# Two PSUM banks for MLP outputs and two for attention tiles, and w_out loaded right behind w_in

## The chip, the cores and the metric

The kernel runs on one core of one Trainium2 chip. The metric is the device time of one execution in microseconds; the median of several executions counts. The core has a matmul engine (TensorE, PE in the profile), VectorE (DVE), ScalarE (ACT), GpSimd (POOL) and SyncE (SP), which here issues all DMAs in one queue. Each engine takes its own instructions in the order in which they were written.

## The reference

Two layers in a row. The first is a linear attention with a decay per channel, for 4 sequences of 768 steps and 8 heads of 48 channels; the second is an MLP over its 3072 rows of 384 values.

```python
for t in range(S):                                  # attention, per batch b and head h
    cur = np.einsum('bhd,bhe->bhde', u[None] * kt, vt)
    y[:, :, t] = np.einsum('bhd,bhde->bhe', rt, state + cur)
    state = wt[:, :, :, None] * state + np.einsum('bhd,bhe->bhde', kt, vt)
x = attn_out.transpose(0, 2, 1, 3).reshape(B * S, H * D)
h = x @ w_in                                        # 384 -> 2048
r = np.maximum(h, 0.0)
g = s * (r * r) + b
return (g @ w_out).astype(np.float32)               # 2048 -> 384
```

## The kernel before

**Tiling.** The steps are cut into chunks of 128, so there are 24 chunks: chunk n is steps `n // 4` of sequence `n % 4`, and they are done in this order. Two chunks make one MLP tile T of 256 rows, so there are 12 tiles. Matmuls run in bf16 with sums in fp32.

**A chunk of attention** is a row of small steps that go from engine to engine. Its r, k, v, w come by four DMAs (`load`). ACT takes the logarithm of w (`ln`); PE sums it along the steps (`cum`, bank pair A); ACT takes the exponents (`expo`, and `lam` for the state); VectorE multiplies r and k by them (`mult`, tile `prd`); PE transposes (`trans`, a bank of pool B), ACT copies the result out (`tevac`, tile `RK`); PE forms the 128x128 products (`mt`, bank pair A), VectorE masks them (`mask`); PE sums the output (`ymm`, pool B) and the state's increment (`dmm`, pool B); VectorE adds the diagonal part (`yevac`, tile `x_sb`) and the state (`supd`); PE transposes x (`xtr`, pool B) and ACT copies it (`xevac`, tile `xT`). GpSimd prepares the diagonal part, v in bf16 and the state's scale.

**A tile of the MLP** is eight groups of MLP-in (`g1`, six matmuls each into one of two h banks), a relu on ACT (`relu`, a ring of four `rh` tiles), a square (`square`, on ACT or VectorE by the letters of `SQE`, and on VectorE for the first two tiles), and eight parts of MLP-out (`g2`, four matmuls each; four parts fill one o bank), which VectorE evacuates with s and the bias term (`oevac`). The bias term, b times the column sums of w_out, is made once: 16 matmuls (`colsum`, tile `cs_ps`, an o bank) and a copy on ACT (`bconst`).

**PSUM** has eight banks: A takes two, B three, h two, o one.

**Weights** come in four pieces of w_in and four of w_out, 768 KB each, in fp32, and are cast to bf16 by the engines that the letters of `CIE` and `COE` name.

**The order** is not written by hand. The class `Plan` holds every step with an engine, a cost in us, the steps it needs, the rings it takes a place in and a priority; `order()` plays the steps forward and gives out the one that could start first. The instructions are then written in that order. SP takes its steps strictly by priority: the priority of chunk n's loads is 10 n + 0 to 3, that of w_in `WIN_AT`, that of w_out `WOUT_AT`. `slack` is time that the planner adds to what an attention step on PE waits for (from chunk 6 on), so more of it puts more other PE work between a producer and its consumer. Steps marked `port` on VectorE and GpSimd are not laid beside each other. Until 28 us the gaps on PE are filled with idle matmuls (`warm_ps`).

Of the kernel before, what the change touches and what calls it, by code (L numbers as in the profile page):

```python
# [14 lines left out]

SHOW = None
WIN_AT = 35.0
WOUT_AT = 45.0
CIE = 'APAP'
COE = 'APAP'  # L20
VBE = 'P'
WARM = 28.0
SQE = 'DAA'
SQT = 2
MSL = 0.1
SLACK = 1.0


class Plan:
# [9 lines left out]
    def add(self, name, eng, occ, fn, args=(), deps=(), takes=(), prio=0.0,  # L39
            lat=0.12, port=False, dma=0.0, slack=0.0):  # L40
        self.ops[name] = dict(
            name=name, eng=eng, occ=occ, fn=fn, args=args, deps=list(deps),
            takes=list(takes), prio=prio, lat=lat, port=port, dma=dma,
            slack=slack, n=len(self.ops),
        )
# [64 lines left out]
def kernel(  # L110
# [15 lines left out]
    B, H, S, D = r.shape  # L126
# [23 lines left out]
        tc.tile_pool(name="psA", bufs=1, space=bass.MemoryType.PSUM)  # L150
    )
    psB = ctx.enter_context(
        tc.tile_pool(name="psB", bufs=3, space=bass.MemoryType.PSUM)
    )
    psH = ctx.enter_context(
        tc.tile_pool(name="psH", bufs=2, space=bass.MemoryType.PSUM)
    )
    psO = ctx.enter_context(
        tc.tile_pool(name="psO", bufs=1, space=bass.MemoryType.PSUM)
    )  # L160

    ctx.enter_context(tc.manual_schedule())
# [20 lines left out]
    XTB = 6  # L183
# [12 lines left out]
    xT = [None] * NT  # L196
    gT = [None] * NT
# [338 lines left out]
    def sq_eng(T, i):  # L536
        return "ACT" if SQE[(T * NQ + i) % len(SQE)] == "A" and T >= SQT else "DVE"

# [45 lines left out]
    def colsum():  # L584
        ps = psO.tile([128, d_model], FP32, name="cs_ps", tag="o")
        for ft in range(FT):
# [9 lines left out]

    pl = Plan(
        dict(w=8, rk=8, v=8, lw=NLW, prd=NPR, E=2, RK=3, M=3, vb=6, yd=6, x=4,
             cd=4, rkp=2, rku=2, l2=5, A=1, B=3, h=2, o=1, gT=3, xT=XTB, rh=4,
             o_sb=4, wst=4, stmp=2)  # L600
    )
    add = pl.add

    CAST = dict(A=("ACT", 1.4), P=("POOL", 1.45), D=("DVE", 0.9))

    def cast(letter, out, in_):
        if letter == "A":
            nc.scalar.copy(out=out, in_=in_)  # L608
        elif letter == "P":
            nc.gpsimd.tensor_copy(out=out, in_=in_)  # L610
        else:
            nc.vector.tensor_copy(out=out, in_=in_)
# [4 lines left out]
    def cast_out(i):  # L617
        cast(COE[i], w_out_sb[i], w_out_st[i])

# [11 lines left out]
    for n in range(N):  # L631
# [3 lines left out]
        P = 10.0 * n  # L635
        SL = SLACK if n > 5 else 0.0
        add(("ln", n), "ACT", 0.45, ln, (n,), [("load", n, 0)] + ([("ln", n - 1)] if n else []),
# [4 lines left out]
            [("rku", [("cd", n)])], P, port=True)  # L642
        e = CAST[VBE[n % len(VBE)]][0]
        add(("vb", n), e, 0.48, castv, (n,), [("load", n, 3)],
            [("vb", [("ymm", n)] + ([("dmm", n)] if keep else []))], P,
            port=e == "POOL")
# [45 lines left out]
    for T in range(NT):  # L692
        P = BIG + 10 * T
        for i in range(NQ):
# [6 lines left out]
                P, lat=0.2, slack=MSL if T > 1 else 0.0)  # L701
            add(("relu", T, i), "ACT", 0.52, relu, (T, i), [("g1", T, i)],
                [("rh", [("sq", T, i)])], -BIG + P)
            e = sq_eng(T, i)
# [32 lines left out]
    for i in range(NPIECE):  # L737
        add(("li", i), "SP", 0.8, load_win, (i,), [], [("wst", [("ci", i)])],
            WIN_AT + 0.1 * i, dma=2.15)
        add(("lo", i), "SP", 0.8, load_wout, (i,), [], [("wst", [("co", i)])],  # L740
            WOUT_AT + 0.1 * i, dma=2.15)
        e, t = CAST[CIE[i]]
        add(("ci", i), e, t, cast_in, (i,), [("li", i)], [], 20.0, port=e == "POOL")
        e, t = CAST[COE[i]]
        add(("co", i), e, t, cast_out, (i,), [("lo", i)], [], 45.0, port=e == "POOL")


    nc.vector.memset(logws[0], 0.0)
# [61 lines left out]
```

## Time and profile before

| | |
|---|---|
| median of 3 runs | 211.35 us (211.01 to 212.12) |
| the profiled execution | 210.94 us, of it the span 209.0 us |
| PE, ACT busy | 192.6 us (92%), 151.7 us (73%) |
| VectorE, GpSimd busy | 126.3 us (60%), 117.7 us (56%) |
| mean granted clock of PE | 0.992 |
| read from HBM, written | 25.36 MB, 4.72 MB |

The span runs from the first to the last instruction of the profiled execution; the time measured for it is 1.94 us longer. Busy times are sums over instructions; matmuls are pipelined and overlap, so PE's is read by stage, with its waits, and not as a share alone. The chain of waits follows the work that ended last back to the start: each row is its start, its length and what it was. In the rows of busy time by stage the columns are the stretch and its length, the busy time of PE, PEld (weight loads), DVE, ACT and POOL with the number of instructions, the granted clock, the DMA share and GB/s. In a row of the timeline, what stands in square brackets is the idle time of the engine before it and what ended it.

### The profile page before, as it was taken

Reading aid. Unit: us, or ns where it says so; the run is one execution under the profiler, and the core shown is the slowest. Engines: PE = TensorE matmul, PEld = TensorE weight load, DVE = VectorE, ACT = ScalarE, POOL = GpSimd, SP = SyncE. Lnnn points to the kernel's source line nnn. Section 1 sums busy time; section 2 is a strip of 40 time slices with the busy share of each in tenths; the row PEclk is TensorE's granted clock in tenths of the full one; section 3 lists DMA queues with packets and bytes.
Section 4 is the critical chain, followed back from the end, with each engine's and each line's share of the span. In section 5 each row is a group of like instructions: output and inputs, shape, how many; then the busy total and the mean of one; then the engine's idle time right before and its main releaser. Section 6 shows DMA issues by size and latency. Waiting matters only on the chain.

```text
span 209.0 us, 5056 instructions
## 1 busy us (share of the span) xinstructions
PE 192.6 (92%) x2008; PEld 143.8 (69%) x2008; DVE 126.3 (60%) x193; ACT 151.7 (73%) x272; POOL 117.7 (56%) x146
## 2 busy tenths in 40 slices
PE   2999688969999989999999899999999999999992
PEld 1767466744668767787687677876876877777650
DVE  5278659883777776687767757867456463611131
ACT  3256687963459989989699799896996998769000
POOL 3779727557999889899979989946100000000000
PEclk9999999996999999999999999999999999999999
DMA  7999998999999999998999999101102010111122
GB/s 132 170 199 150 334 331 188 378 230 198 188 176 198 156 193 199 214 228 180 219 194 205 207 218 184 43 3 38 41 0 76 3 35 6 38 41 39 38 75 77
DMA packets 107464, 30.41 MB, mean 145 GB/s; under 512 B 100656, under 2 KB 105904, under 8 KB 107440
## 3 DMA queue, kind: packets, MB, share of 16 engines
q1 hardware_dynamic: 107440, 30.09, 69.5%
q8 instruction: 15, 0.25, 0.5%
q14 instruction: 9, 0.07, 0.1%
HBM read 25.36 MB, written 4.72 MB: 144 GB/s over the span
## 4 chain that ended last, share of the span: by engine, by line
PE 73%; DMA 11%; SPq 9%; DVE 2%; ACT 1%; issue 1%; POOL 1%; ACTq 0%
PE o_ps L558 28%; PE h_ps L520 26%; SPq L216 7%; DMA wo_st<-in_moe_w_out_dram 6%; DMA wt<-in_w_dram 5%; PE trps L331 4%; PE mt_ps L356 3%; PE o_psh L558 2%; PE y_ps L393 2%; PE y_ps L384 1%; PE cums L272 1%; PE cums L275 1%; PE xt_ps L471 1%; SPq L491 1%; PE d_ps L409 1%; DVE o_sb L568 1%
## 5 line engine op out<-in xcount | busy, mean ns | idle before, releaser
L520 PE MATMUL h_ps<-xT,w_in 128*128 128x256 bf16 x576 | 75.4, 273 | 2.8 <-ACT w_in L608 1.3
L558 PE MATMUL o_ps<-w_out,gT 128*128 128x384 bf16 x352 | 67.6, 332 | 1.5 <-DVE o_sb L568 1.1
L533 ACT ACTIVATE rh<-h_ps 128x512 bf16<-128x512 f32 x96 | 56.0, 595 | 11.2 <-PE h_ps L520 11.0
L520 PEld LDWEIGHTS <-w_in 128*128 128x128 bf16 x576 | 53.4, 98 | 13.2 <-issue 1.9
L558 PEld LDWEIGHTS <-gT 128*128 128x128 bf16 x384 | 37.0, 99 | 22.4 <-issue 3.8
L543 ACT ACTIVATE gT<-rh 128x512 bf16<-128x512 bf16 x54 | 34.0, 630 | 1.7
L368 DVE TENSOR_TENSOR mt_sb<-mt_ps,tri_strict 128x1024 bf16<-128x1024 f32 x24 | 29.3, 1221 | 6.6 <-PE mt_ps L356 6.5
L304 DVE TENSOR_TENSOR prd<-rkt,E 128x768 bf16<-128x768 f32 x24 | 24.2, 1008 | 14.3 <-ACT E L294 13.2
L545 DVE TENSOR_TENSOR gT<-rh 128x512 bf16<-128x512 bf16 x42 | 24.4, 593 | 12.7 <-ACT rh L533 12.6
L346 ACT COPY RK<-trps 128x1024 bf16<-128x1024 bf16 x24 | 24.0, 1001 | 7.8 <-PE trps L331 7.8
L228 POOL TENSOR_TENSOR rkp<-rkt 128x384 f32<-128x384 f32 x24 | 24.1, 1005 | 5.6 <-DMA rkt<-in_k_dram 5.4
L239 POOL TENSOR_TENSOR rku<-rkp,u_bc 128x384 f32<-128x384 f32 x24 | 25.0, 1040 | 0.8
L568 DVE SCALAR_TENSOR_TENSOR o_sb<-o_ps,s_bc,bconst 128x384 f32<-128x384 f32 x22 | 13.5, 616 | 18.8 <-PE o_ps L558 18.5
L294 ACT ACTIVATE E<-cums 128x768 bf16<-128x768 f32 x24 | 19.3, 805 | 6.1 <-PE cums L280 6.1
L259 POOL TENSOR_TENSOR yd<-vt,cd 128x384 bf16<-128x384 f32 x24 | 22.0, 916 | 2.2 <-DVE cd L253 1.8
L423 DVE TENSOR_TENSOR x_sb<-y_ps,yd 128x384 bf16<-128x384 f32 x24 | 13.3, 555 | 12.0 <-PE y_ps L393 12.0
L318 POOL TENSOR_TENSOR l<-lam,par 128x8 f32<-128x8 f32 x20 | 15.7, 787 | 5.6 <-ACT lam L298 5.2
L460 POOL TENSOR_TENSOR st<-stmp,l 128x384 bf16<-128x384 bf16 x16 | 14.3, 895 | 6.3 <-DVE stmp L451 6.2
L768 PE MATMUL warm_ps<-warm_sb 128*128 128x256 bf16 x96 | 13.9, 293 | 4.0 <-DVE warm_sb L763 4.0
L223 ACT ACTIVATE logw<-wt 128x384 bf16<-128x384 f32 x24 | 12.6, 526 | 6.1 <-DMA wt<-in_w_dram 4.0
L253 DVE TENSOR_REDUCE cd<-rku 128x8 f32<-128x384 f32 x24 | 13.1, 546 | 6.0 <-POOL rku L239 5.9
L486 ACT COPY xT<-xt_ps 128x384 bf16<-128x384 bf16 x24 | 11.4, 474 | 4.8 <-PE xt_ps L471 4.7
(51 smaller groups left out, 191.9 us busy)
## 6 DMA issues: line engine op xcount, KB each, us to landing
wt<-in_w_dram SPq DMA_DIRECT2D x24, 192.0 KB, 4.6
rkt<-in_r_dram SPq DMA_DIRECT2D x24, 192.0 KB, 4.3
rkt<-in_k_dram SPq DMA_DIRECT2D x24, 192.0 KB, 4.5
vt<-in_v_dram SPq DMA_DIRECT2D x24, 192.0 KB, 4.4
out_dram<-o_sb SPq DMA_DIRECT2D x24, 192.0 KB, 3.1
wi_st<-in_moe_w_in_dram SPq DMA_DIRECT2D x4, 768.0 KB, 8.1
wo_st<-in_moe_w_out_dram SPq DMA_DIRECT2D x4, 768.0 KB, 8.9
u_bc<-in_u_dram SPq DMA_DIRECT2D x1, 192.0 KB, 4.5
```

The costliest lines, as they stand in the source:

```text
L228: nc.gpsimd.tensor_tensor(out=rkp, in0=c["rk"][:, 0].rearrange("t h d -> t (h d)"), in1=c["rk"][:, 1].rearrange("t h d -> t (h d)"), op=AL ...
L239: nc.gpsimd.tensor_tensor(out=rku.rearrange("t h d -> t (h d)"), in0=c["rkp"], in1=u_bc, op=ALU.mult)
L259: nc.gpsimd.tensor_tensor(out=yd, in0=c["v"], in1=c["cd"].unsqueeze(2).to_broadcast([128, H, D]), op=ALU.mult,)
L294: nc.scalar.activation(out=E, in_=ps[:, :, 0:HD], func=AF.Exp)
L304: nc.vector.tensor_tensor(out=prd[:, :, :, 0:D].rearrange("t x h d -> t (x h) d"), in0=c["rk"].rearrange("t x h d -> t (x h) d"), in1=c["E ...
L346: nc.scalar.copy(out=RK, in_=c["trps"])
L368: nc.vector.tensor_tensor(out=m.rearrange("s g p t -> s (g p) t"), in0=c["mt_ps"].rearrange("s g p t -> s (g p) t"), in1=tri_strict.unsque ...
L520: nc.tensor.matmul(ps[:, f, :], lhsT=w_in_sb[ft // FPP][:, kt, (ft % FPP) * 128 : (ft % FPP + 1) * 128], rhs=xT[T][:, kt, :], start=(f == ...
L533: nc.scalar.activation(out=rh, in_=hs[T, i], func=AF.Relu)
L543: nc.scalar.activation(out=g, in_=rh, func=AF.Square)
L545: nc.vector.tensor_tensor(out=g, in0=rh, in1=rh, op=ALU.mult)
L558: nc.tensor.matmul(ps, lhsT=gT[T][:, ft, tt * 128 : (tt + 1) * 128], rhs=w_out_sb[ft // FPP][:, ft % FPP, :], start=(ft == 0), stop=(ft == ...
```

## The change

Four things are changed. `WOUT_AT` goes from 45 to 36, so w_out is loaded ahead of chunk 4 and not behind it, and `COE` has VectorE cast all its pieces. `SQE` goes from one square in three on VectorE to one in two (from tile 2 on). Pool B gives one bank to pool o, and the planner's rings follow. `SLACK` goes from 1.0 to 0.3, and the planner now keeps VectorE's casts apart from GpSimd's steps.

```diff
-WOUT_AT = 45.0
+WOUT_AT = 36.0
 CIE = 'APAP'
-COE = 'APAP'
+COE = 'DDDD'
...
-SQE = 'DAA'
+SQE = 'DA'
...
-SLACK = 1.0
+SLACK = 0.3
...
-        tc.tile_pool(name="psB", bufs=3, space=bass.MemoryType.PSUM)
+        tc.tile_pool(name="psB", bufs=2, space=bass.MemoryType.PSUM)
...
-        tc.tile_pool(name="psO", bufs=1, space=bass.MemoryType.PSUM)
+        tc.tile_pool(name="psO", bufs=2, space=bass.MemoryType.PSUM)
...
-             cd=4, rkp=2, rku=2, l2=5, A=1, B=3, h=2, o=1, gT=3, xT=XTB, rh=4,
+             cd=4, rkp=2, rku=2, l2=5, A=1, B=2, h=2, o=2, gT=3, xT=XTB, rh=4,
...
-    CAST = dict(A=("ACT", 1.4), P=("POOL", 1.45), D=("DVE", 0.9))
+    CAST = dict(A=("ACT", 1.4), P=("POOL", 1.45), D=("DVE", 0.88))
...
-        add(("ci", i), e, t, cast_in, (i,), [("li", i)], [], 20.0, port=e == "POOL")
+        add(("ci", i), e, t, cast_in, (i,), [("li", i)], [], 20.0, port=e != "ACT")
...
-        add(("co", i), e, t, cast_out, (i,), [("lo", i)], [], 45.0, port=e == "POOL")
+        add(("co", i), e, t, cast_out, (i,), [("lo", i)], [], 45.0, port=e != "ACT")
```

SP's list of DMAs around the weights, before (the first row is w_in, the next four are chunk 4, then w_out):

```order
L491 DMA wi_st<-in_moe_w_in_dram 128x3x512 x4
L216 DMA wt<-in_w_dram 128x8x48
L216 DMA rkt<-in_r_dram 128x8x48
L216 DMA rkt<-in_k_dram 128x8x48
L216 DMA vt<-in_v_dram 128x8x48
L501 DMA wo_st<-in_moe_w_out_dram 128x4x384 x4
```

and after:

```order
L491 DMA wi_st<-in_moe_w_in_dram 128x3x512 x4
L501 DMA wo_st<-in_moe_w_out_dram 128x4x384 x4
L216 DMA wt<-in_w_dram 128x8x48
L216 DMA rkt<-in_r_dram 128x8x48
L216 DMA rkt<-in_k_dram 128x8x48
L216 DMA vt<-in_v_dram 128x8x48
```

The four w_out pieces have changed places with the four loads of chunk 4; the loads of chunk 5 stand behind both in either order.

VectorE at the same place, before: the squares (`gT`) of tiles 0 and 1, with the steps of chunk 4 between them.

```order
L545 TENSOR_TENSOR gT<-rh 128x512 x4
L304 TENSOR_TENSOR prd_106<-rkt,E 128x16x48
L545 TENSOR_TENSOR gT<-rh 128x512 x2
L253 TENSOR_REDUCE cd<-rku 128x8
L545 TENSOR_TENSOR gT<-rh 128x512
L368 TENSOR_TENSOR mt_sb<-mt_ps,tri_strict 128x1024
```

After, from the same four squares on (L612 is the cast of a w_out piece):

```order
L545 TENSOR_TENSOR gT<-rh 128x512 x4
L612 CAST w_out_98<-wo_st 128x1536
L545 TENSOR_TENSOR gT<-rh 128x512 x2
L612 CAST w_out_99<-wo_st 128x1536
L545 TENSOR_TENSOR gT<-rh 128x512 x3
L612 CAST w_out_100<-wo_st 128x1536
L545 TENSOR_TENSOR gT<-rh 128x512 x3
L612 CAST w_out_101<-wo_st 128x1536
L545 TENSOR_TENSOR gT<-rh 128x512 x2
L253 TENSOR_REDUCE cd<-rku 128x8
L304 TENSOR_TENSOR prd_106<-rkt,E 128x16x48
```

The four casts stand between the squares, and chunk 4's `cd` and `prd` have moved behind all of them.

ACT at the same place, before: chunk 4's logarithm (`logw_103`), exponents and transposed copy (`RK`) stand between the relus, and so do two w_out casts.

```order
L533 ACTIVATE rh<-h_ps 128x512 x2
L223 ACTIVATE logw_103<-wt 128x8x48
L533 ACTIVATE rh<-h_ps 128x512 x2
L486 COPY xT<-xt_ps 128x3x128
L294 ACTIVATE E<-cums 128x768
L298 ACTIVATE lam<-cums 128x4
L533 ACTIVATE rh<-h_ps 128x512 x4
L346 COPY RK<-trps 128x1024
L533 ACTIVATE rh<-h_ps 128x512 x2
L608 CAST w_out_98<-wo_st 128x1536
```

After:

```order
L533 ACTIVATE rh<-h_ps 128x512 x4
L486 COPY xT<-xt_ps 128x3x128
L533 ACTIVATE rh<-h_ps 128x512 x10
L594 ACTIVATE bconst<-cs_ps,b_bc 128x384
L223 ACTIVATE logw_103<-wt 128x8x48
L294 ACTIVATE E<-cums 128x768
L298 ACTIVATE lam<-cums 128x4
L223 ACTIVATE logw_104<-wt 128x8x48
```

The relus of tile 1 now run without a step of chunk 4 between them, and chunk 4's logarithm stands behind the copy of the bias term.

## The prediction

> **What bounds the kernel now.** I read the page first, then the chain of waits, then busy time by stage, then the waits of PE.
>
> ```profile
> PE 192.6 (92%) x2008; PEld 143.8 (69%) x2008; DVE 126.3 (60%) x193; ACT 151.7 (73%) x272; POOL 117.7 (56%) x146
> PEclk9999999996999999999999999999999999999999
> ```
>
> PE is the engine to fill. Its clock is whole except in one slice, the tenth (47.0 to 52.3 us).
>
> ```profile
> 34.16 11.56 DMA wo_st<-in_moe_w_out_dram
> 45.77 1.47 POOL w_out L610
> 47.29 0.82 PE cs_ps L587 x4
> 48.14 0.59 ACT bconst L594
> 48.77 4.37 PE o_ps L558 x16
> ...
> 61.83 0.66 PE h_ps L520 x6
> 62.49 0.33 PE mt_ps L356 x8
> ...
> 80.18 0.65 PE o_ps L558 x4
> ...
> 205.03 0.62 DVE o_sb L568
> ```
>
> Up to 48.77 the chain is a load: the last piece of w_out lands at 45.77, is cast on POOL, summed into cs_ps, copied to bconst, and only then does the first output matmul start. From there to 205.03 it is nearly all PE. So whatever starts that PE train earlier moves the end, and whatever makes PE wait inside it moves it back. (x6 is one group of MLP-in, 0.66 us; x4 one part of MLP-out, 0.65 us; the sixteen at 48.77 took 4.37 us where four times 0.65 is 2.6.)
>
> ```profile
> 43.00:48.77 5.77, 3.47 (x25) 1.90 (x23) 3.75 (x5) 3.98 (x7) 2.82 (x3) 0.99 0.93 190
> 48.77:52.10 3.33, 3.33 (x11) 1.62 (x11) 1.42 (x2) 1.23 (x3) 3.03 (x4) 0.50 1.23 197
> ...
> 61.83:150.00 88.17, 86.61 (x999) 67.10 (x997) 62.10 (x94) 78.35 (x148) 74.82 (x90) 1.00 0.86 163
> 150.00:205.05 55.05, 54.98 (x502) 39.85 (x500) 22.32 (x35) 37.46 (x66) 0.00 (x0) 1.00 0.10 37
> ```
>
> Columns: length, busy PE, PEld, DVE, ACT, POOL, granted clock, DMA share, GB/s. Three facts. PE idles 2.3 us of the 5.77 before 48.77. The 3.33 us behind that ran at clock 0.50, so half of it, 1.67 us, was lost. From 61.83 on PE is idle only 1.56 + 0.07 us. The last row also says that the tail holds nothing to win.
>
> **The change, part by part.**
>
> *Loads.* SP's list now has the four w_out pieces right behind w_in, ahead of chunk 4 (chunks count from 0); nothing else moves ahead of chunk 5. What landed when:
>
> ```profile
> 31.82 1.75 POOL L610 CAST w_in<-wi_st 128x1536 bf16<-128x1536 f32 x1 [3.74 <-DMA wi_st<-in_moe_w_in_dram]
> 32.42 0.52 ACT L223 ACTIVATE logw<-wt 128x384 bf16<-128x384 f32 x1 [1.29 <-DMA wt<-in_w_dram]
> 33.62 1.48 PE L520 MATMUL h_ps<-xT,w_in 128*128 128x256 bf16 x12
> 34.31 1.05 POOL L228 TENSOR_TENSOR rkp<-rkt 128x384 f32<-128x384 f32 x1 [0.75 <-DMA rkt<-in_k_dram]
> 43.32 1.47 ACT L608 CAST w_out<-wo_st 128x1536 bf16<-128x1536 f32 x1 [1.38 <-DMA wo_st<-in_moe_w_out_dram]
> 45.77 1.46 POOL L610 CAST w_out<-wo_st 128x1536 bf16<-128x1536 f32 x1 [2.11 <-DMA wo_st<-in_moe_w_out_dram]
> 46.37 0.52 ACT L223 ACTIVATE logw<-wt 128x384 bf16<-128x384 f32 x1 [0.22 <-DMA wt<-in_w_dram]
> 48.08 0.99 POOL L228 TENSOR_TENSOR rkp<-rkt 128x384 f32<-128x384 f32 x1 [0.84 <-DMA rkt<-in_k_dram]
> ```
>
> Pieces of w_out land 2.45 us apart at the end (43.32, 45.77); w_in ended at 31.82. Between them lie 13.95 us, in which 3 MB of w_out and chunk 4 came. At some 2.25 to 2.45 us a piece, w_out by itself takes 9.0 to 9.8, so its last piece lands at 40.8 to 41.6 instead of 45.77: 4.2 to 5.0 us earlier. Chunk 4's w (32.42 now) lands 0.6 us behind it, about 41.7, its k (1.9 later by the rows of chunk 4) about 43.4. Chunk 5 has the same bytes ahead of it as before: w at 46.37, k at 48.08.
>
> *Casts on VectorE.* No row has a VectorE cast. The same tile took 1.47 us on ACT and 1.46 on POOL; the fastest VectorE rate in the trace is a square, 0.407 us for 512 columns, which makes 1.22 for 1536.
>
> ```profile
> L545 DVE TENSOR_TENSOR gT<-rh x42: 407/426/1704, 27.4 to 191.3; 128x512 bf16<-128x512 bf16 x42
> ```
>
> I take 1.2 (the nearest row on that engine) and keep 0.8 and 1.5 as ends, since a copy reads one operand and a square two. The Trainium skill, "VectorE: DVE Perf Modes", The perf-mode tier table, gives 1227 ns for a 2048-column fp32 copy; an estimate from it is 0.92 us, and by it the sum below does not change. The casts stand between squares in VectorE's order, so a late piece holds the squares behind it, and by the ring of four rh tiles the relus. Piece 3 at about 41.2 follows square 13, which ends near 40.7, so the cast ends at 42.4.
>
> *PE until chunk 5.* Its order is now: ten MLP-in groups in a row, colsum, cum of chunk 4, three MLP-out parts, cum of chunk 5. The ten start at 33.62 as now (the last w_in cast ends at 33.57) and take 0.66 to 0.72 each, as each h bank must pass its relu: until about 40.6. Colsum is 16 matmuls at 0.163 (0.65 for four): the first twelve end near 42.5, just behind the last cast, the last four at 43.2. On ACT the Ln of chunk 4 is queued behind bconst: 0.59 + 0.52 puts its end at 44.3. Cum takes 0.43, three parts 1.95: 46.7, and some 0.1 more at each of four hand-overs between engines (0.05 from 45.77 + 1.47 to 47.29): 47.1. Chunk 5's Ln can end no earlier than 46.37 + 0.52 = 46.9, so cum of chunk 5 starts at 47.0 to 47.2 by either way. I take 47.2.
>
> ```profile
> 52.98 0.61 PE L331 MATMUL trps<-identity,prd 128*128 128x128 bf16 x8
> 53.42 0.33 PE L409 MATMUL d_ps<-vb,prd 128*128 128x96 bf16 x4
> 53.59 0.33 PE L272 MATMUL cums<-logw,tri_strict 128*128 128x384 bf16 x1
> ...
> 54.02 2.11 PE L558 MATMUL o_ps<-w_out,gT 128*128 128x384 bf16 x12
> ...
> 57.79 0.37 PE L393 MATMUL y_ps<-vb,mt_sb 128*128 128x48 bf16 x8
> ...
> 59.55 0.33 PE L471 MATMUL xt_ps<-identity,x_sb 128*128 128x128 bf16 x3
> 59.72 2.11 PE L558 MATMUL o_ps<-w_out,gT 128*128 128x384 bf16 x12
> ```
>
> Start to start these give a chunk's PE work: transposes 0.44, d 0.17, cum 0.43, xt 0.17; with mt 0.33 and y 0.4, 1.9 us. At 48.77 the kernel of before has done all of chunk 4 and cum of chunk 5 more than the changed kernel at 47.2 (1.5 + 0.43 = 1.9), which in turn has three MLP-out parts more (1.95). The remaining work is equal, so the start is worth 48.77 - 47.2 = **1.6 us**. A cast of 1.5 us would move the squares and colsum by some 1.4 and leave 0.2.
>
> *The half clock.* It cost 1.67 us. Whether it comes back depends on how busy PE is ahead of it:
>
> ```profile
> 22.40:25.80 3.40, 1.97 (x25) 1.30 (x21) 1.88 (x3) 2.41 (x4) 2.53 (x4) 1.00 1.01 337
> ...
> 44.27:47.67 3.40, 1.36 (x9) 0.63 (x7) 2.48 (x4) 2.40 (x5) 1.46 (x1) 1.00 0.79 149
> ```
>
> 58% busy over 3.4 us (22.4 on) was followed by a whole clock, 40% (44.27 on) by half. After the change PE idles about 1.3 us behind colsum (bconst and Ln) and then runs cum and three parts: in the 3.4 us behind colsum it is busy 2.1, 62%. That is nearest to the stretch that kept its clock, so I count **1.67 us** gained. The Trainium skill, "TensorE: Matmul & The Clock Gate", The HAM clock gate, has the clock halve after an idle window of about 3.4 us. This trace differs: no PE wait there passes 1.7 us, and the clock halved all the same; by the rule to the letter there is no half clock after the change, the same 1.67.
>
> *The train behind it.* PE's waits from 62 us on:
>
> ```profile
> PE o_ps L558 <- DVE o_sb L568: 1.1, 2, 0.5
> PE h_ps L520 <- ACT xT L486: 0.5, 2, 0.2
> ```
>
> The second o bank takes away the 1.1. Against that, four kinds of attention tiles (transposes, y, d, xt) now share two banks, and with a smaller SLACK the planner puts less PE work between a producer and its consumer. Counted in the two orders at the prices above, a reuse of a B bank has under 1 us to spare beyond its evacuation at 12 places (2 before), and an xt behind its y at 14 (8 before). No row prices these. Lower end: nothing, and the 1.6 us go (-1.6). Upper end: each of the some 70 reuses from chunk 6 on waits 0.1 us, +7. Before, the places with 0.5 to 1 us to spare show no wait, which lies nearest to the low end; I put +1.8 for new waits, net **+0.2**.
>
> *Squares.* 14 go from ACT to VectorE:
>
> ```profile
> L543 ACT ACTIVATE gT<-rh 128x512 bf16<-128x512 bf16 x54 | 34.0, 630 | 1.7
> L545 DVE TENSOR_TENSOR gT<-rh 128x512 bf16<-128x512 bf16 x42 | 24.4, 593 | 12.7 <-ACT rh L533 12.6
> ```
>
> ACT loses 14 x 0.630 = 8.8 us of work, VectorE gains 14 x 0.593 = 8.3. Neither sets the end: PE hardly waits for either, and VectorE has 26 us free of the 88 to 150. Cost nothing, with PE's MLP work as cover; without it, 8.3 us over the 18 later chunks would be 0.5 us a chunk. The two casts taken off POOL (2.9 us) and ACT (2.9) lay beside the load wait and count there alone.
>
> *Sum:* -1.6 - 1.67 + 0.2 = -3.1, taken as -3.0 against the profiled execution's 210.94 (209.0 span plus 1.94 around it): 207.9. That execution lies 0.41 under the median of 211.35, so for the median 208.3.
>
> **The rivals.**
>
> *The clock halves again.* The 62% is my estimate, and one more wait of 0.5 us brings it to 47%. Then the 1.67 stay lost: -1.4, 209.9. A slow cast (1.5 us) ends in the same place. Chance 0.20.
>
> *The gain is given back in the train.* New waits of 4.4 to 5.2 us instead of 1.8 make 210.9 to 211.7, no change. The port: squares read two operands from SBUF, and their time went from a median of 0.426 to 1.704 at the worst. The Trainium skill, "GPSIMD Engine Reference", Specifications, says that GpSimd's SBUF interfaces are shared with VectorE instructions that have two SBUF inputs, which speaks against moving squares there, and the spread of that row fits it. If each of the 14 costs POOL 0.3 us in the stretch where it is 74.82 of 88.17 busy, that is 4 of its 13 free us: hidden, unless its yd and st come late. Chance 0.14.
>
> *Slower: two banks are too few.* One mechanism: a transpose, y, d or xt waits on PE until the tile two before it is evacuated, and all MLP work queued behind waits too. It decides from 3.27 + 1.6 + 1.06 = 5.9 us of new waits on, 0.085 at each of 70 reuses. For it: evacuations queue behind relus on ACT (78.35 of 88.17 busy). Against: all but some 12 of them have over 1 us to spare. At the upper end above, 7 us, it gives 213.5. Chance 0.10.
>
> *More.* The train runs without waits: -1.6 - 1.67 - 1.6, 206.5. Chance 0.06.
>
> The forecast itself, 207 to 209.5, has 0.50.
>
> **Numbers.** 0.5%, about what a measurement of this kernel can tell from no change, is 1.06 us. Faster by more: 0.50 + 0.06 + 0.15 of the first rival's 0.20 = 0.71. Within: 0.05 + 0.13 = 0.18. Slower: 0.10 + 0.01 = 0.11. The range leaves out about 0.1 at either end: from 206.2, just past a train without waits, to 211.6, past the case that gives all back.
>
> **What would show it.** The last w_out cast ends near 42.4 and the first o_ps of an output tile starts near 45 (48.77 now); PEclk has no 6; cum of chunk 5 at 47.2; the first MLP-in group behind the MLP-out parts starts near 59.7 (61.83). Waits of PE for RK, stmp, x_sb or xT that sum to over 4 us behind 62, or a clock of 0.5 near 47, or VectorE casts of 1.5 us, would make it wrong.

## The result, and the profile after

The changed kernel takes 204.97 us against 211.59 us in the same series, a ratio of 0.9698 (0.9649 to 0.9747): about 6.4 us less, where 3.0 were forecast and 206.2 was the lower end of the range. Its profiled execution has 204.84 us with a span of 203.0, against 210.94 and 209.0.

The page, busy time and granted clock:

```profile
PE 191.0 (94%) x2008; PEld 143.3 (71%) x2008; DVE 134.6 (66%) x211; ACT 143.0 (70%) x256; POOL 114.3 (56%) x144
PEclk9999999999999999999999999999999999999999
```

The slice at half clock is gone. The chain of waits, its pieces around the start of the PE train and at its end:

```profile
36.49 6.99 DMA rkt<-in_k_dram
43.62 1.01 POOL rkp L228
44.69 1.01 POOL rku L239
46.20 0.96 DVE prd L304
47.99 1.95 PE o_ps L558 x12
...
59.51 1.42 PE h_ps L520 x12
...
193.96 5.21 PE o_psh L558 x32
```

The last load on the chain is now k of chunk 4 and no longer a piece of w_out. The timeline of that stretch:

```profile
40.22 0.96 DVE L612 CAST w_out<-wo_st 128x1536 bf16<-128x1536 f32 x1 [0.24 <-DMA wo_st<-in_moe_w_out_dram]
...
44.38 2.11 PE L558 MATMUL o_ps<-w_out,gT 128*128 128x384 bf16 x12
...
45.32 0.53 ACT L223 ACTIVATE logw<-wt 128x384 bf16<-128x384 f32 x1
...
46.33 0.33 PE L272 MATMUL cums<-logw,tri_strict 128*128 128x384 bf16 x1
...
59.44 1.49 PE L520 MATMUL h_ps<-xT,w_in 128*128 128x256 bf16 x12
```

The last w_out cast ends at 41.18 (47.24 before), the first MLP-out part starts at 44.38 (48.77), MLP-in of tile 2 at 59.44 (61.83). By then two MLP-out parts and one `mt`, 1.63 us, are done that before came later, so the start gained 2.39 + 1.63 = 4.0 us in this pair of executions. PE's last matmul ends 5.9 us earlier (199.2 against 205.05); the other 1.9 came out of the train. Its busy time by stage, before and after:

```profile
62.00:205.05 143.05, 141.42 (x1497) 106.80 (x1494) 84.29 (x129) 115.81 (x212) 74.65 (x90) 1.00 0.57 114
```

```profile
62.00:199.10 137.10, 136.82 (x1457) 103.75 (x1454) 92.54 (x139) 107.02 (x196) 75.60 (x91) 1.00 0.59 119
```

PE idled 1.63 us there before and 0.28 now: 1.35 of the train's 1.9 us are waits that went, and no row here accounts for the other 0.5. One wait is left in the whole train:

```profile
PE h_ps L520 <- ACT rh L533: 0.3, 1, 0.3
```

### The profile page after: what moved, and what is told of

Same layout as the page of the kernel before. It is cut to its first block, busy times and chain, and to the rows that moved or that the text cites. A ratio compares the mean times of both kernels' runs of the same rounds, so it can differ in the third digit from the quotient of the medians.

```text
span 203.0 us, 5059 instructions
## 1 busy us (share of the span) xinstructions
PE 191.0 (94%) x2008; PEld 143.3 (71%) x2008; DVE 134.6 (66%) x211; ACT 143.0 (70%) x256; POOL 114.3 (56%) x144
## 4 chain that ended last, share of the span: by engine, by line
PE 73%; SPq 11%; DMA 9%; DVE 2%; POOL 2%; issue 1%; ACT 0%; DVEq 0%; POOLq 0%
PE o_ps L558 28%; PE h_ps L520 26%; SPq L216 9%; DMA wi_st<-in_moe_w_in_dram 5%; PE trps L331 4%; DMA rkt<-in_k_dram 3%; PE mt_ps L356 3%; PE o_psh L558 3%; PE y_ps L393 2%; PE y_ps L384 2%; PE xt_ps L471 2%; PE d_ps L409 2%; PE cums L272 1%; PE cums L275 1%; SPq L491 1%
## 5 line engine op out<-in xcount | busy, mean ns | idle before, releaser
L520 PE MATMUL h_ps<-xT,w_in 128*128 128x256 bf16 x576 | 73.9, 272 | 1.3 <-ACT w_in L608 0.8
L558 PE MATMUL o_ps<-w_out,gT 128*128 128x384 bf16 x352 | 66.4, 326 | 0.0
L558 PEld LDWEIGHTS <-gT 128*128 128x128 bf16 x384 | 35.6, 98 | 18.8
L545 DVE TENSOR_TENSOR gT<-rh 128x512 bf16<-128x512 bf16 x56 | 28.5, 522 | 12.5 <-ACT rh L533 12.5
L228 POOL TENSOR_TENSOR rkp<-rkt 128x384 f32<-128x384 f32 x24 | 25.7, 1071 | 15.4 <-DMA rkt<-in_k_dram 15.3
L304 DVE TENSOR_TENSOR prd<-rkt,E 128x768 bf16<-128x768 f32 x24 | 26.4, 1106 | 6.8 <-ACT E L294 6.0
L543 ACT ACTIVATE gT<-rh 128x512 bf16<-128x512 bf16 x40 | 25.2, 630 | 1.3
L460 POOL TENSOR_TENSOR st<-stmp,l 128x384 bf16<-128x384 bf16 x16 | 17.8, 1112 | 4.9 <-DVE stmp L451 4.9
L768 PE MATMUL warm_ps<-warm_sb 128*128 128x256 bf16 x96 | 14.7, 306 | 4.0 <-DVE warm_sb L763 4.0
L223 ACT ACTIVATE logw<-wt 128x384 bf16<-128x384 f32 x24 | 12.4, 522 | 3.1 <-DVE warm_sb L763 2.0
L331 PE MATMUL trps<-identity,prd 128*128 128x128 bf16 x192 | 14.6, 219 | 0.0
```

The costliest lines, as they stand in the source:

```text
L228: nc.gpsimd.tensor_tensor(out=rkp, in0=c["rk"][:, 0].rearrange("t h d -> t (h d)"), in1=c["rk"][:, 1].rearrange("t h d -> t (h d)"), op=AL ...
L304: nc.vector.tensor_tensor(out=prd[:, :, :, 0:D].rearrange("t x h d -> t (x h) d"), in0=c["rk"].rearrange("t x h d -> t (x h) d"), in1=c["E ...
L331: nc.tensor.matmul(ps[:, x * HP + p, :], lhsT=c["prd"][:, x, 2 * p : 2 * p + 2, :].rearrange("t h d -> t (h d)"), rhs=identity, is_transpo ...
L520: nc.tensor.matmul(ps[:, f, :], lhsT=w_in_sb[ft // FPP][:, kt, (ft % FPP) * 128 : (ft % FPP + 1) * 128], rhs=xT[T][:, kt, :], start=(f == ...
L543: nc.scalar.activation(out=g, in_=rh, func=AF.Square)
L545: nc.vector.tensor_tensor(out=g, in0=rh, in1=rh, op=ALU.mult)
```

## The experiments

Theories are named in the expectations. In short: A, the load order brings the start's gain by itself; B, the casts are needed for it; C, what decides is the order that the planner makes; D and E, the banks act by themselves or through that order; F, the order can be judged beforehand by its tight places; G, it cannot. All ratios are to the kernel before, on the same chip. The changed kernel itself was timed only in the four executions of the result. Where its 0.9698 is set beside another ratio, its interval of half a percent either way comes on top, so a difference under some 0.6% says nothing. The kernel before had a median of 211.59 us there and of 210.2 to 210.7 in the later series.

| run | what differs | median us | ratio (95%) |
|---|---|---|---|
| e1 | before, idle matmuls in colsum | 210.36 | 0.9995 (0.9974 to 1.0017) |
| e2 | before, load order alone | 227.4 | 1.0787 (1.0752 to 1.0822) |
| e3 | before, load order and casts | 218.44 | 1.0359 (1.0327 to 1.0391) |
| e4 | changed, load order and casts back | 208.16 | 0.9889 (0.9853 to 0.9925) |
| e5 | changed, SLACK back | 209.22 | 0.9942 (0.9909 to 0.9975) |
| e6 | changed, banks back | 210.13 | 0.997 (0.9947 to 0.9992) |
| e7 | changed, squares back | 209.61 | 0.9955 (0.9928 to 0.9981) |
| e8 | before, SLACK 0.3 alone | 213.0 | 1.0126 (1.0087 to 1.0164) |
| e9 | changed, its order, pools back | 214.91 | 1.022 (1.0182 to 1.0258) |
| e10 | before, its order, new pools | 211.65 | 1.0061 (1.003 to 1.0092) |
| e11 | changed, its order, squares back | 208.36 | 0.991 (0.9875 to 0.9945) |
| e12 | changed, its order, casts back | 206.03 | 0.9799 (0.9762 to 0.9836) |
| e13 | changed, SLACK 0.2 | 204.95 | 0.9729 (0.9699 to 0.9758) |
| e14 | changed, SLACK 0.35 | 207.09 | 0.9835 (0.9807 to 0.9864) |
| e15 | changed, last w_in cast on VectorE | 207.75 | 0.9856 (0.9828 to 0.9885) |
| e16 | changed, two w_in casts on VectorE | 205.84 | 0.9773 (0.9745 to 0.9801) |

### Is the half clock worth its time?

```diff
         for ft in range(FT):
+            if ft == 12:
+                fill = psH.tile([128, TOK], FP32, name="fill_ps", tag="h")
+                for _ in range(12):
+                    nc.tensor.matmul(
+                        fill, lhsT=warm_sb[:, 0:128], rhs=warm_sb, start=True, stop=True
+                    )
             nc.tensor.matmul(
                 ps,
                 lhsT=ones,
```

> The kernel before, with 12 idle matmuls written into colsum ahead of its last four, where PE waits 1.63 us for the last w_out cast; nothing else moves. If the half clock behind 48.77 comes from the low PE activity ahead of it, the clock stays whole, the first sixteen MLP-out matmuls take 2.6 us instead of 4.37 and the time falls by 1.5 to 1.8 us (209.8 to 210.1). If the clock halves for another reason (by length of a single wait, or whatever precedes 44), it halves here too: no change, 211.6.

The clock stayed whole and the median did not move. The ratio alone says little of what a half clock costs: 3.33 us of it lower the mean clock over 209 us by 0.008, to 0.992, and only 4 of the 17 executions of the kernel before in this series lie there or lower (none of the 12 with idle matmuls). The timeline says more:

```profile
48.28 2.76 PE L558 MATMUL o_ps<-w_out,gT 128*128 128x384 bf16 x16 [0.27 <-ACT bconst L600]
51.26 0.62 PE L331 MATMUL trps<-identity,prd 128*128 128x128 bf16 x8 [0.22 <-DVE prd L304]
...
55.75 0.62 PE L331 MATMUL trps<-identity,prd 128*128 128x128 bf16 x8 [0.23 <-DVE prd L304]
...
56.88 0.37 PE L393 MATMUL y_ps<-vb,mt_sb 128*128 128x48 bf16 x8 [0.34 <-DVE mt_sb L368]
...
60.88 0.81 PE L520 MATMUL h_ps<-xT,w_in 128*128 128x256 bf16 x6
```

The first sixteen matmuls now pass in 2.76 us instead of 4.37, and behind them PE waits for chunks 5 and 6. From the first MLP-out part to MLP-in of tile 2 it is 12.6 us, 13.06 with the half clock, for the same work: the slow matmuls had covered waits on attention, and the half clock cost about 0.5 us and not 1.67. Over the 72 executions of the kernel before that stand beside these runs, those with a mean clock up to 0.992 (19) have a median span of 209.2, the rest (53) 208.4. So, read by its mean clock, it comes in about a quarter of them and goes with 0.8 us there; whether those executions differ in something else as well is not shown.

### The start alone

```diff
-WOUT_AT = 45.0
+WOUT_AT = 36.0
```

> The kernel before with w_out loaded right behind w_in and nothing else changed (casts on ACT and POOL, three B banks, one o bank). Theory A, the load order makes the gain of the start by itself: the first MLP-out part comes at 44.5 to 45.5, the clock stays whole, and the time falls by 3 to 4 us (207.6 to 208.6), casts of 1.47 us costing some 0.5. Theory B, the casts on VectorE are needed, since casts on ACT hold up the relus and those on POOL do not: the start gains 2 us or less. Theory C, the new order that the planner makes behind it decides: waits of PE behind 62 us change by more than 2 us either way.

```diff
-COE = 'APAP'
+COE = 'DDDD'
```

> Load order and casts on VectorE, the rest as before (three B banks, one o bank, one square in three on VectorE, SLACK 1.0). Theory A: the whole gain of the start, 4.0 us, and the train as before: 207.6. Theory B: 1 us or more better than load order alone. Theory C: the train's waits differ from the 1.6 us of before by more than 2 us.

Theory A fell hard: load order alone is 7.9% slower, and with the casts still 3.6%. Of theory B it holds that the casts on VectorE matter: they bring back 9 of the 17 us. The start itself worked: with both, the first MLP-out part starts at 45.2. The loss is in the train: with both, PE's waits from 62 us on sum to 8.9 us (1.6 before), the largest two of them

```profile
PE o_ps L558 <- DVE o_sb L568: 3.8, 6, 1.1
PE h_ps L520 <- ACT xT L486: 1.8, 4, 0.6
```

ACT's timeline, the copies of x of chunks 5, 6 and 7, with load order and casts:

```profile
56.06 0.48 ACT L486 COPY xT<-xt_ps 128x384 bf16<-128x384 bf16 x1
76.67 0.48 ACT L486 COPY xT<-xt_ps 128x384 bf16<-128x384 bf16 x1 [2.62 <-PE xt_ps L471]
78.69 0.48 ACT L486 COPY xT<-xt_ps 128x384 bf16<-128x384 bf16 x1 [1.54 <-PE xt_ps L471]
```

and in the changed kernel:

```profile
58.39 0.48 ACT L486 COPY xT<-xt_ps 128x384 bf16<-128x384 bf16 x1
65.92 0.47 ACT L486 COPY xT<-xt_ps 128x384 bf16<-128x384 bf16 x1
71.18 0.46 ACT L486 COPY xT<-xt_ps 128x384 bf16<-128x384 bf16 x1
```

The planner put 20 us between chunks 5 and 6. MLP tile 3 needs chunks 6 and 7, so PE runs out of MLP work before they are there:

```profile
69.84 0.81 PE L558 MATMUL o_ps<-w_out,gT 128*128 128x384 bf16 x4 [0.71 <-DVE o_sb L568]
...
79.22 0.82 PE L520 MATMUL h_ps<-xT,w_in 128*128 128x256 bf16 x6 [0.57 <-ACT xT L486]
```

Between 62 and 90 us it idles 2.2 us here and nothing in the changed kernel. A train that starts 4 us earlier also needs chunk 7 some 4 us earlier.

### The rest alone, and each part taken back

The changed kernel with the load order and the casts of before (the `CAST` and `port` lines too):

```diff
-WOUT_AT = 36.0
+WOUT_AT = 45.0
-COE = 'DDDD'
+COE = 'APAP'
```

> The changed kernel with the load order and the casts as before: only the banks, the squares and SLACK changed. Theory A: the start as before (first MLP-out part near 48, half clock behind it) and the train without its waits: a gain of 1.6 to 2.2 us, 209.4 to 210. By theory C (the planner's order for these very settings together removed the waits) it gains nothing, or loses: 211 to 214.

It gains 1.1% (0.7 to 1.5), 2.3 us, close to theory A's figure for the train; theory C's is excluded. From 62 us on PE has one wait left:

```profile
PE cums L272 <- ACT lam L298: 0.2, 1, 0.2
```

The half clock that theory A kept is not in its profile, so not all of the gain need be the train's. By difference the start is worth the other 4 us, but only in company of the rest.

```diff
-SLACK = 0.3
+SLACK = 1.0
```

> The changed kernel with SLACK 1.0 again, all else as changed. Theory C, now split: C1, SLACK is what lets the planner fit the chunks behind the new start (with 1.0 it puts about 20 us of PE work between the x of chunk 5 and that of chunk 6, as in the kernel with load order and casts alone): PE idles 3 us or more behind 62 us and the time is 209 to 216. C2, the second o bank does it (PE waited 3.8 us for o_sb with load order and casts alone): SLACK costs little, 205 to 207, and PE's waits for o_sb stay at nothing.

```diff
-        tc.tile_pool(name="psB", bufs=2, space=bass.MemoryType.PSUM)
+        tc.tile_pool(name="psB", bufs=3, space=bass.MemoryType.PSUM)
...
-        tc.tile_pool(name="psO", bufs=2, space=bass.MemoryType.PSUM)
+        tc.tile_pool(name="psO", bufs=1, space=bass.MemoryType.PSUM)
...
-             cd=4, rkp=2, rku=2, l2=5, A=1, B=2, h=2, o=2, gT=3, xT=XTB, rh=4,
+             cd=4, rkp=2, rku=2, l2=5, A=1, B=3, h=2, o=1, gT=3, xT=XTB, rh=4,
```

> The changed kernel with three B banks and one o bank again. C2: PE waits for o_sb for 3 us or more and the time is 208 to 212. C1: the attention steps follow each other as closely as in the changed kernel, only the o waits of some 1 us come back, 205.5 to 207.

```diff
-SQE = 'DA'
+SQE = 'DAA'
```

> The changed kernel with one square in three on VectorE again, 14 more squares of 0.63 us on ACT. If ACT holds up PE (91% busy from 62 to 150 us before), relus come late: PE waits for rh, RK or xT for 2 us or more and the time is 207 to 210. If only the planner's order matters, it goes by that order: the x of chunk 7 stands further behind that of chunk 6 than in the changed kernel, which gives 206 to 209 too, but with the waits on attention tiles and not on rh. If neither matters, 205.

The kernel before with one line of the change:

```diff
-SLACK = 1.0
+SLACK = 0.3
```

> The kernel before with SLACK 0.3 and nothing else. C1: the closer order helps by itself, PE's 1.6 us of waits behind 62 us go or change places, 209 to 210.5. C2: the one o bank keeps its waits for o_sb, and places with under 0.3 us to spare (9 instead of 6 behind chunk 5) add some: 210.5 to 213.

Each part taken back loses 2.4 to 2.7% of the time, nearly all that was gained, and SLACK 0.3 alone makes the kernel before 1.3% slower: the parts do not add up. C1 and C2 both hold in part: with SLACK back PE waits 3.9 us from 62 us on and none of it for o_sb, as C1 says; with the banks back the time lies where C2 put it, but only 1.4 us of waits are for o_sb, half of what C2 asked. With the squares back 3.5 us are for xT and none for rh; that profile also has a clock of 0.94 between 62 and 90 us. SLACK 0.3 alone leaves 1.9 us for o_sb. With SLACK 1.0, PE's waits between 62 and 90 us are on attention and on its relus:

```profile
77.06 0.34 PE L471 MATMUL xt_ps<-identity,x_sb 128*128 128x128 bf16 x3 [0.71 <-DVE x_sb L423]
78.31 0.62 PE L331 MATMUL trps<-identity,prd 128*128 128x128 bf16 x8 [0.92 <-DVE prd L304]
...
82.89 0.82 PE L520 MATMUL h_ps<-xT,w_in 128*128 128x256 bf16 x6 [1.69 <-ACT rh L533]
```

These runs cannot tell what a part does by itself, since the planner makes another order for each. The next four keep the order to the letter.

### The same order, one resource changed

The changed kernel with the pools as before and the planner's rings as changed:

```diff
-        tc.tile_pool(name="psB", bufs=2, space=bass.MemoryType.PSUM)
+        tc.tile_pool(name="psB", bufs=3, space=bass.MemoryType.PSUM)
...
-        tc.tile_pool(name="psO", bufs=2, space=bass.MemoryType.PSUM)
+        tc.tile_pool(name="psO", bufs=1, space=bass.MemoryType.PSUM)
```

> The changed kernel with its order of instructions kept to the letter, but the pools as before: three B banks and one o bank; the planner still counts two and two. Theory D, the second o bank is worth what the order spends on it: in this order an output tile's first part stands with 0 to 0.17 us of PE work behind the last part of the tile before at 11 of 21 places, and at each PE would now wait some 0.65 us for o_sb: 6 to 8 us, 211 to 213. Theory E, the banks matter only through the order that the planner makes: 205 to 206.5.

PE's waits:

```profile
PE o_ps L558 <- DVE o_sb L568: 8.7, 12, 1.0
```

Theory D: the changed order lets one output tile follow the other at 11 places, and with one o bank PE waits for it 12 times, 8.7 us in all, somewhat more than the 6 to 8 that were expected. Theory E falls.

The reverse, the new pools in the order of before, the planner's rings left at three and one:

```diff
-        tc.tile_pool(name="psB", bufs=3, space=bass.MemoryType.PSUM)
+        tc.tile_pool(name="psB", bufs=2, space=bass.MemoryType.PSUM)
...
-        tc.tile_pool(name="psO", bufs=1, space=bass.MemoryType.PSUM)
+        tc.tile_pool(name="psO", bufs=2, space=bass.MemoryType.PSUM)
```

> The kernel before with its order kept, but the pools of the change: two B banks, two o banks. The 1.1 us of waits for o_sb go. Two places of B come to under 0.1 us to spare (y12 behind tr13, d6 behind tr6) and cost 0.3 us each at most. Theory D and my step on the train: 209.5 to 210.5 against 210.5. If two B banks are too few by themselves: 212 or more.

It is 0.6% slower, not faster. The o waits are gone, but PE waits 0.9 us for transposes behind the copy of x (`trps` behind `xT`), which came in their place; from 62 us on its waits sum to 2.5 us, 1.6 before. A second o bank brings nothing in an order that was not made for it.

Squares on the engines of before, order kept:

```diff
-        if sq_eng(T, i) == "ACT":
+        if "DAA"[(T * NQ + i) % 3] == "A" and T >= SQT:
```

> The changed kernel with its order kept, but one square in three on VectorE as before: each square stands at the same place of the program, on the other engine. If ACT's load is what the squares are about, its 14 squares of 0.63 us hold up relus and copies of attention, and PE waits for rh, RK or xT: 206.5 to 209. If the squares acted through the planner's order alone: 205 to 206.

2.1% slower than the changed kernel by the ratios (0.991 against 0.9698): ACT's load holds PE up. Its busy time from 62 us to PE's end:

```profile
62.00:203.20 141.20, 138.81 (x1460) 104.11 (x1457) 86.07 (x126) 112.39 (x210) 74.42 (x91) 1.00 0.59 115
```

PE idles 2.39 us in it (0.28 in the changed kernel), for relus and x. Its span is 4.0 us longer; of what lies ahead of 62 most is a wait for a w_in cast (2.0 us against 0.8), which the squares do not touch. So about 2.1 us are theirs in this pair of traces.

Casts on ACT and POOL in turn, order kept:

```diff
-        cast(COE[i], w_out_sb[i], w_out_st[i])
+        cast("APAP"[i], w_out_sb[i], w_out_st[i])
```

> The changed kernel with its order kept, but the w_out casts on ACT and POOL in turn, where POOL has nothing else from 32 to 43 us. Those on ACT stand between the relus and hold two of them up by 1.47 us each: MLP-in of tile 1 ends up to 2 us later, and colsum with it. If the place of chunk 4's k (43.6 us) and w of chunk 5 sets the end of the start, half of it is hidden: 205.5 to 207. If the casts on VectorE are worth what they seem in the kernels with the planner's own order, more: 208 or above.

1.0% slower than the changed kernel by the ratios. Those on ACT hold up the relus, and MLP-in of tile 1 waits for them twice, 1.04 us each:

```profile
36.23 3.81 PE L520 MATMUL h_ps<-xT,w_in 128*128 128x256 bf16 x30 [1.04 <-ACT rh L533]
...
41.09 1.47 PE L520 MATMUL h_ps<-xT,w_in 128*128 128x256 bf16 x12 [1.04 <-ACT rh L533]
```

### Can the order be judged beforehand?

For every consumer on PE behind chunk 3 I counted in the written order how much PE work stands between it and its producer on PE, and took off what the step between them takes on its own engine by the profile's rows (1.0 us for a copy of transposes, 1.22 for a mask, and so on). Where under 0.3 us is left, the place is tight. The kernel before has 6 tight places, the changed one none; load order alone 22, with casts 14; SLACK back 8. Then I took four orders by this count. First, SLACK 0.2:

```diff
-SLACK = 0.3
+SLACK = 0.2
```

> The changed kernel with SLACK 0.2: another order, no place behind chunk 3 where a consumer on PE stands less than 0.3 us beyond what the steps ahead of it take (the changed kernel: none; the kernel before: 6 places, 1.6 us below that line in sum). Theory F, these places set the train: 204 to 206, PE idle under 1 us behind 62 us. Theory G, 0.3 is a point that was found by trial and the count says nothing: 207 to 211.

```diff
-SLACK = 0.3
+SLACK = 0.35
```

> The changed kernel with SLACK 0.35: 7 such places, 2.4 us below the line in sum, as many as with SLACK 1.0 (8 places, 2.3 us, 209.2 us). Theory F: 208 to 210.5, PE idle 3 us or more behind 62. Theory G: so small a step of SLACK changes little, 204.5 to 206.

```diff
-CIE = 'APAP'
+CIE = 'APAD'
```

> The changed kernel with the last w_in cast on VectorE instead of POOL. The cast itself ends about 0.5 us earlier. Its order has 10 such places, 4.0 us in sum. Theory F: 209 to 212. Theory G or H (the load of the engines sets the time): 204 to 205.5.

```diff
-CIE = 'APAP'
+CIE = 'ADPD'
```

> The changed kernel with the second and the last w_in cast on VectorE. Its order has no such place, and MLP-in of tile 0 need not wait for the last cast so long (0.8 us of PE's waits at the w_in casts). Theory F: 203.5 to 205, the fastest so far. Theory G: anything between 204 and 211.

The two orders without a tight place are at 0.973 and 0.977, those with 7 and 10 at 0.984 and 0.986. Theory F holds in direction, in four orders. The sizes do not: 2.1 and 2.8 us more than SLACK 0.2 (medians of the same series), where 3 to 7 were expected, and e16 is not the fastest. Theory G, that the count says nothing, would need one of the untight orders slow; none was, though 205.84 us for e16 lies in its span too. So the count is supported and not proven. Of PE's 2.5 us of waits with SLACK 0.35 behind 62 us, the second and third row below, 1.3 us, stand at such places, and the first is for relus:

```profile
PE h_ps L520 <- ACT rh L533: 0.8, 2, 0.6
PE cums L272 <- DVE mt_sb L368: 0.7, 1, 0.7
PE y_ps L384 <- ACT RK L346: 0.6, 1, 0.6
```

No version beat the changed kernel clearly: SLACK 0.2 is level with it.

## Why the prediction was wrong

The direction was right and the gain half of what came. The signs named for the start came nearly as forecast: the last w_out cast ended at 41.18 (forecast 42.4), the first MLP-out part began at 44.38 (45), tile 2 at 59.44 (59.7). The step that failed is the train behind it. By its steps:

- **Loads.** Nearly right for what the sum used of w_out: the last piece was there at 40.2 (forecast 40.8 to 41.6) and k of chunk 4 at 43.6 (43.4). The last w_in cast began at 30.63 and not at 31.82 as before; over the traces with this load order and that cast on GpSimd it lies between 30.0 and 32.1, so part of this is chance. Wrong for chunk 5: its logarithm started at 45.32, so w landed at least 1.05 us before the 46.37 that I held fixed.
- **Casts.** 0.96 us where I took 1.2; the estimate of 0.92 from the Trainium skill ("VectorE: DVE Perf Modes", The perf-mode tier table) agrees with this row. It did not matter to the sum, as said. That a slow cast would cost the start about 1.4 us was of the right kind: 1.0% in e12, though through the relus behind ACT's casts.
- **PE until chunk 5.** The ten MLP-in groups started at 32.78 (forecast 33.62) and cum of chunk 5 at 46.33, not 47.2: 2.4 us gained by this step and not 1.6.
- **The half clock** went, as forecast, but the term was mis-sized: it cost about 0.5 us (12.6 against 13.06 us in e1) and not 1.67. I had quoted how long the slow matmuls took, and not asked what PE would wait for next if they were fast. That the stretch between the first MLP-out part and tile 2 still gave about 1.6 us has for the most part another reason: before, it held 10.8 us of work in 13.06; now, from 46.33 to 59.44, it holds 12.4 in 13.11. With chunks 4 and 5 side by side behind the weights, PE has MLP-out parts to fill their gaps. That the number came out near the term is luck. The Trainium skill's rule on the idle window ("TensorE: Matmul & The Clock Gate", The HAM clock gate: half clock after an idle window of about 3.4 us) changes nothing in this.
- **The train** is the term that failed most: +0.2 forecast, -1.9 measured. I put +1.8 us on new waits, from places with under 1 us to spare. They did not wait: PE's idle time behind 62 us fell from 1.63 us to 0.28. By e13 to e16 the line lies nearer to 0.3 us, and by that line the same count says the opposite: 6 places before, none after.
- **Squares**: "cost nothing" was wrong. e11 prices them at 2 to 4.5 us in this order. ACT, busy 78.35 of 88.17 us, was not free cover; with the 14 squares back on it in the same order, PE waits for relus and for x again.
- **The bank**: I gave the second o bank the 1.1 us of waits that the trace shows. e9 shows 8.7 in the new order. A wait in the trace of before prices a resource only in the order of before.

Of the rivals, the halved clock did not come. Too few B banks by themselves was the slower rival; e10 shows some of it in the old order, but the planner's new order keeps every B place clear. What I called "More" (206.5) was the nearest, and still short by the loads and the work that filled the gaps. It had PE's waits go, as they did, but named nothing that would make them go beside the bank.

What stays open: how much of the 4 to 5 us that SLACK is worth in company sits in the tight places and how much in chunk 7 being late, and why tight places cost less in e14 and e15 than in e5.

## What to carry to other kernels

Where a planner sets the order, the parts of a change are not terms of a sum: price a resource by keeping the written order and changing that resource alone, and price the order by what stands between producer and consumer in it. Starting the critical engine earlier pays only if the work that feeds it later is due earlier too; find the next thing it will run out of before counting the gain. And before a slow stretch is counted as a loss, look at what the engine would wait for if it were fast.

## What the runs showed of the hardware

The half clock comes in some executions of the same program and not in others: 19 of 72 have a mean clock up to 0.992, which is what 3.33 us at half clock leave of 209 us. With idle matmuls in the gap ahead of it none of 12 has. A VectorE cast of 128x1536 from fp32 to bf16 took 0.96 us where ACT took 1.47 and GpSimd 1.46, and a square on VectorE between 0.41 and 1.7 us in the kernel before, 0.422 on average behind 150 us, where GpSimd is idle, and 0.626 (five squares) between 90 and 120, where GpSimd is busy 28.38 of 30 us.
